# Sums of squares of ten chunks by products of the channels with themselves, instead of Square and add

## The chip, the cores and the metric

The kernel runs on one core of one Trainium2 chip. The metric is the device time of one execution in microseconds. The time before is the median of three runs. One execution was recorded by the hardware profiler, and all rows of the trace below come from that one. A core has TensorE (PE in the rows; PEld is its weight load), VectorE (DVE), ScalarE (ACT), GpSimd (POOL) and SyncE, whose queue (SPq) issues most of the transfers. Each works through its own list of instructions in order, and they wait for one another by semaphores.

## The reference, cut to what matters

```python
B, N, C = 4, 5056, 256
qn = q / (np.linalg.norm(q, axis=1, keepdims=True) + 1e-06)
kn = k / (np.linalg.norm(k, axis=1, keepdims=True) + 1e-06)
s = kn.transpose(0, 2, 1) @ qn / tau
a = softmax of s over its last axis
out = v @ a                        # [B, N, C], then as [B * N, C] into:
logits = x @ w_gate                # one of E = 8 experts for each token
h = np.maximum(xe @ w1[e], 0.0)    # F = 1024
out[mask] = gate_w[mask, None] * (h @ w2[e])
```

For each batch the kernel needs the 256 x 256 product of the channels of k with those of q over all 5056 tokens, and, for the norms, the sum of squares over the tokens of each of the 512 channels of q and k.

## The kernel before

**Attention.** A batch's q and k come in 20 chunks (`nch`) of 256 padded tokens: one chunk is a tile `raw` of 128 partitions x 2 tokens x 512 channels in fp32, 256 of q and 256 of k (L190, L191). For each chunk the two accumulators `sp[0]` and `sp[1]` get the product of k and q (L204 to L216), in one of two ways. A chunk that is not split goes to TensorE as fp32: four matmuls of 128 x 256, each with its own weights (L209). A chunk that is split is first cast by ScalarE to a rounded half (L173), VectorE subtracts that from the chunk for the second half (L174), and eight matmuls of the halves follow (L213, L214). Beside that, ScalarE squares the chunk into `sq` (L202), and VectorE adds `sq` to the running sum `ssq` (L203); of chunk 0 the square goes to `ssq` itself (L200). After the last chunk four small matmuls with a column of ones sum `ssq` over the partitions into `ntp` (L223), VectorE clips it into `ss` (L229), and from it come the norms, the softmax and the 256 x 256 matrix of the batch, with the gate's weights behind it.

Then come ten groups (`G`) of 512 tokens. The values of a group are loaded (`vraw`, L308), eight fp32 matmuls into four tiles `px` give its rows and logits (L322 in the first batch), ScalarE copies each `px` into `xg` and squares it for a scale (L327, L329), ScalarE and VectorE write the rows as two halves (L343, L344), a short chain on VectorE picks the expert (`r_m` to `r_ex`, L352 to L373), TensorE counts places (`rtp`, L380 and L383), and four indirect transfers on POOL's queue scatter the rows to their expert (L402).

**Weights.** `weights()` loads the 16 matrices of the experts (L117, L122; the last into `wraw`), forms the diagonal of a product of each with itself on TensorE for its scale (`gram`, 16 matmuls of 128 x 128 in bf16, L137, and L140 to L144), and splits each in two halves with one large operation on ScalarE (L105) and one on VectorE (L106).

**Blocks.** When the first six groups (`CUT`) of batch 0 are scattered, `table(0)` counts the rows of each expert (`ctp`, L462, and some 25 small operations on VectorE to `c_tb`), and blocks of 256 rows of one expert start. The block's address is read from `c_tb` on SyncE's queue, the rows come by a transposing transfer (`xT`, L543) and their factors by a small one (`mt`, L545, used by VectorE at L586 for `b_fac`); then come 48 matmuls `hp` (L571) and 48 `y` (L594). The rest of the kernel is a row of such blocks, with the attention of the later batches dealt out between them.

**Order of the work.** At L658 to L662 one loop deals out the opening: batch 0 (`first`), the weights, and from step 23 on one chunk of batch 1 (`second`) in every step, ten chunks in all; chunks 10 to 19 of batch 1 run between blocks. Of batch 1, chunk 0 and chunks 14 to 19 are split, 1 to 13 are not. The framework then orders each engine's instructions by its own planning, so that the order on an engine is not that of the code; it is fixed when the program is built.

**Buffers.** Chunks and values of these stages share the three buffers of the tag `raw`; `px` and `gram` share three PSUM buffers (`hp`); `hl`, `sq`, `soft` and `wraw` share two buffers (tag `hl`); `ps_y` holds the two PSUM buffers `y0` and `y1` of a block's result, which batch 0 used for its `sp` before.

Of the kernel before, what the change touches and what calls it, by code (L numbers as in the profile page):

```python
# [10 lines left out]
F32 = mybir.dt.float32  # L11
F32R = mybir.dt.float32r
F16 = mybir.dt.float16
# [3 lines left out]
ALU = mybir.AluOpType  # L17
# [3 lines left out]
P = 128  # L21
# [9 lines left out]
CUT = 6  # L31
# [30 lines left out]
def attention_then_experts(ctx, tc, q, k, vT, tau, w_gate, w1, w2, kc, out):  # L62
    nc = tc.nc
    sync, act, vec, pool, pe = nc.sync, nc.scalar, nc.vector, nc.gpsimd, nc.tensor

    one = ctx.enter_context(tc.tile_pool(name="one", bufs=1))
    work = ctx.enter_context(tc.tile_pool(name="work", bufs=2))
    tiny = ctx.enter_context(tc.tile_pool(name="tiny", bufs=2))
# [3 lines left out]
    ps_y = ctx.enter_context(tc.tile_pool(name="ps_y", bufs=1, space=bass.MemoryType.PSUM))  # L72
# [91 lines left out]
    NATIVE = 14  # L164
# [9 lines left out]
        vec.tensor_tensor(out=hl[:, 1], in0=raw, in1=hl[:, 0], op=ALU.subtract)  # L174
        return hl

    def attention(b, s_split, x_split, acc):

# [1 line left out]
        sp = [pool_.tile([P, 2, C], F32, tag=tag, name=f"sp{c}") for c, (pool_, tag) in enumerate(acc)]  # L182
        ssq = one.tile([P, 2, 512], F32, tag="a_l", name="ssq")
        nch = len(s_split)
        for ch in range(nch):

            tag, bufs = (("raw", RAW), ("rows", 3), ("xg", 2), ("raw", RAW), ("rows", 3))[ch % 5 if b == 0 else 0]
            raw = work.tile([P, 2, 512], F32, tag=tag, name="raw", bufs=bufs)
            sl = slice(2 * ch, 2 * ch + 2)
            sync.dma_start(out=raw[:, :, 0:C], in_=qv[b][:, sl, :])  # L190
            load = sync.dma_start(out=raw[:, :, C:512], in_=kv[b][:, sl, :])  # L191
            if b == 0:
                last_load[0] = load.ins
            if s_split[ch]:
                hl = split(raw)
                sq = raw
            else:
                sq = work.tile([P, 2, 512], F32, tag="hl", name="sq", bufs=2)
            if ch == 0:
                act.activation(ssq, raw, AF.Square)  # L200
            else:
                act.activation(sq, raw, AF.Square)  # L202
                vec.tensor_tensor(out=ssq, in0=ssq, in1=sq, op=ALU.add)  # L203
            for j in range(2):  # L204
                first, last = ch == 0 and j == 0, ch == nch - 1 and j == 1
                for c in range(2):
                    kc0 = C + c * P
                    if not s_split[ch]:
                        pe.matmul(  # L209
                            sp[c][:, 0, :], raw[:, j, kc0 : kc0 + P], raw[:, j, 0:C], start=first, stop=last  # L210
                        )
                        continue
                    pe.matmul(sp[c], hl[:, 0, j, kc0 : kc0 + P], hl[:, :, j, 0:C], start=first, stop=False)  # L213
                    pe.matmul(  # L214
                        sp[c][:, 1, :], hl[:, 1, j, kc0 : kc0 + P], hl[:, 0, j, 0:C], start=False, stop=last
                    )  # L216
            yield 2 * 640

# [2 lines left out]
        tp = ps_t.tile([P, 512], F32, tag="tp", name="ntp")  # L221
# [3 lines left out]
        def four(name):  # L225
            return tiny.tile([P, 4], F32, name=name)

        ss, y, h = four("n_ss"), four("n_y"), four("n_h")
        vec.tensor_scalar(out=ss, in0=tp[:, 0:4], scalar1=1e-30, scalar2=None, op0=ALU.max)  # L229

        vec.tensor_scalar(
            out=y.bitcast(I32), in0=ss.bitcast(I32), scalar1=-0.5, scalar2=float(0x5F3759DF), op0=ALU.mult, op1=ALU.add
# [34 lines left out]
        for c in range(2):  # L267
            vec.scalar_tensor_tensor(
                out=s2[:, c, :], in0=sums[c], scalar=rn[:, 2 + c : 3 + c], in1=rq, op0=ALU.mult, op1=ALU.mult
# [8 lines left out]
        for c in range(2):  # L278
            vec.tensor_scalar(
                out=a_x[:, c, 0:C], in0=s2[:, c, :], scalar1=z[:, c : c + 1], scalar2=None, op0=ALU.mult  # L280
            )

        tp = ps_t.tile([P, 512], F32, tag="tp", name="atp")
# [7 lines left out]
        tp = ps_t.tile([P, 512], F32, tag="tp", name="gtp")  # L291
        for c1 in range(2):
            for c2 in range(2):
                pe.matmul(
                    tp[:, c1 * E : (c1 + 1) * E], aT[:, c2, c1 * P : (c1 + 1) * P], wg[:, c2, :],
                    start=(c2 == 0), stop=(c2 == 1),
# [9 lines left out]
        for g in range(G):  # L306
            raw = work.tile([P, 2, 512], F32, tag="raw", name="vraw", bufs=RAW)
# [4 lines left out]
            ss = tiny.tile([P, T], F32, name="x_ss")  # L312
            for t in range(T):
# [22 lines left out]
                out=sc.bitcast(I32), in0=ss.bitcast(I32), scalar1=-0.5, scalar2=float(0x5F3759DF) + 4.92 * TWO23,  # L336
                op0=ALU.mult, op1=ALU.add,
# [26 lines left out]
            last = g == G - 1  # L364
# [248 lines left out]
    def run(gen):  # L613
        for _ in gen:
            pass
# [8 lines left out]
    normal = [(ps_a, "acc")] * 2  # L624
    wts = weights()
    first = attention(0, [False] * nch, False, [(ps_y, "y0"), (ps_y, "y1")])
    second = attention(1, [i == 0 or i >= NATIVE for i in range(nch)], True, normal)
    take(first, 2)


# [58 lines left out]
    look(0)  # L689
    look(1)  # L690
    run(first)
    for n, (s, i) in enumerate(stages):
        while s not in tables:
            next(side)
        look(n)
        look(n + 1)
        for k, _ in enumerate(block(s, tables[s], i, *ahead.pop(n))):
            if k == 0:
                look(n + 2)
            want = np.interp(n + (k + 1) / 8, marks, amounts)  # L700
            while side is not None and s_at < want:
                ns = next(side, None)
                if ns is None:
                    side = None
                else:
                    s_at += ns
# [41 lines left out]
```

## Time and profile before

| | |
|---|---|
| time, median of 3 runs | 1219.38 us (1216.57 to 1224.59) |
| the profiled execution's own time | 1222.09 us, of it 1220.2 us from the first to the last instruction |
| PE busy | 1161.4 us (95%) |
| PE's weight loads | 1025.4 us (84%) |
| DVE busy | 904.7 us (74%) |
| ACT busy | 645.3 us (53%) |
| POOL busy | 383.5 us (31%) |
| PE's mean granted clock | 0.988 of full speed |

Busy shares are means over the whole span, and the stages differ: the opening, up to about 160 us, holds batch 0's attention, the split of the weights and ten chunks of batch 1, and after it come the blocks. Times in rows of the timeline are counted from the span's start. The matmuls' ends are modelled in the trace, so the spacing of their starts says more than their length does. One fp32 matmul stands in the trace as two records.

### The profile page before, as it was taken

How to read it: one execution, taken by the hardware profiler on the slowest of the kernel's cores; microseconds unless marked ns; L12 is line 12 of the kernel's file. 1: busy time of each engine (PE TensorE's matmuls, PEld its weight loads, DVE VectorE, ACT ScalarE, POOL GpSimd, SP SyncE). 2: the span in 40 equal slices, each digit the busy share in tenths (PEclk: the TensorE clock that was granted, in tenths of full speed). 3: DMA queues.
4: the chain of work that ended last, by engine and by line, in shares of the span. 5: the costliest groups of instructions: out<-in, count | busy, mean ns of one | idle time of the engine just before them, and what ended most of it. 6: DMA issues, size and time to landing. Idle time of an engine off the chain costs nothing. (4 is left out here: it accounts for less than half of the span.)

```text
span 1220.2 us, 28272 instructions
## 1 busy us (share of the span) xinstructions
PE 1161.4 (95%) x10212; PEld 1025.4 (84%) x10212; DVE 904.7 (74%) x2384; ACT 645.3 (53%) x1362; POOL 383.5 (31%) x366
## 2 busy tenths in 40 slices
PE   8888789988899999999999999999999999999998
PEld 7767578877788889888888888889888888888897
DVE  5689789677787777777788777777676656656886
ACT  5388864776655545666655545666523332332322
POOL 0027651444521122444441112444431111111111
PEclk9889999999999999999999999999999999999999
DMA  9989685444355433444354534433241222221221
GB/s 302 351 278 316 156 206 136 117 122 131 103 137 127 136 84 96 119 121 109 94 152 114 138 87 96 114 114 79 62 114 48 53 53 53 49 45 42 43 50 33
DMA packets 196830, 145.91 MB, mean 120 GB/s; under 512 B 117580, under 2 KB 176337, under 8 KB 196688
## 3 DMA queue, kind: packets, MB, share of 16 engines
q1 hardware_dynamic: 181296, 102.48, 34.2%
q0 software_dynamic: 15392, 41.60, 9.5%
q8 instruction: 81, 1.33, 0.5%
q14 instruction: 61, 0.50, 0.1%
HBM read 80.03 MB, written 43.29 MB: 101 GB/s over the span
## 5 line engine op out<-in xcount | busy, mean ns | idle before, releaser
L571 PE MATMUL hp<-xT,wp 128*128 128x256 f16 (+1 forms) x4320 | 452.1, 263 | 5.1 <-issue 1.4
L594 PE MATMUL y<-wp,ht 128*128 128x256 f16 x3888 | 450.3, 273 | 6.4 <-DVE ht L579 2.7
L594 PEld LDWEIGHTS <-ht 128*128 128x128 f16 x3888 | 372.4, 98 | 68.1 <-issue 10.4
L571 PEld LDWEIGHTS <-wp 128*128 128x128 f16 x4320 | 383.8, 98 | 52.1 <-issue 6.1
L605 POOL DMA_INDIRECT out<-o,mt x162 | 184.3, 1138 | 649.6 <-ACT o L603 612.4
L559 DVE COPY wp<-W 128x1024 f16 x720 | 297.6, 428 | 111.9 <-PE y L594 64.4
L578 ACT ACTIVATE ht<-hp 128x512 f16<-128x512 f32 x324 | 191.2, 595 | 201.3 <-PE hp L571 162.8
L579 DVE SCALAR_TENSOR_TENSOR ht<-hp,ht 128x512 f16<-128x512 f32 x324 | 220.4, 685 | 36.8 <-ACT ht L578 31.5
L402 POOL DMA_INDIRECT xs<-rows,r_si x160 | 182.3, 1139 | 145.8 <-ACT xjunk L329 50.1
L603 ACT ACTIVATE o<-y,b_fac 128x256 f32<-128x256 f32 x162 | 68.8, 469 | 175.5 <-PE y L594 161.3
L325 PE MATMUL px<-a_h,hl 128*128 128x264 f32 x480 | 99.1, 296 | 1.3 <-ACT xg L327 0.8
L343 ACT ACTIVATE rows<-xg,x_sc 128x256 f16<-128x256 f32 x160 | 69.2, 498 | 35.7 <-issue 16.3
L325 PEld LDWEIGHTS px<-a_h,hl 128*128 128x128 f32 x480 | 79.1, 188 | 4.1 <-issue 1.8
L174 DVE TENSOR_TENSOR hl<-raw,hl 128x1024 fp32r<-128x1024 f32 x47 | 57.4, 1221 | 30.7 <-ACT hl L173 30.7
L213 PE MATMUL sp<-hl 128*128 128x512 f32 x188 | 72.4, 418 | 1.0 <-DVE hl L174 1.0
L173 ACT CAST hl<-raw 128x1024 fp32r<-128x1024 f32 x47 | 49.1, 1044 | 45.0 <-PE sp L214 40.0
L209 PE MATMUL sp<-raw 128*128 128x256 f32 x264 | 64.0, 394 | 9.0 <-DMA raw<-in_k 9.0
L202 ACT ACTIVATE raw<-raw 128x1024 f32<-128x1024 f32 x44 | 46.6, 1058 | 44.6 <-DVE hl L174 42.5
L344 DVE SCALAR_TENSOR_TENSOR rows<-xg,x_sc,rows 128x256 f16<-128x256 f32 x160 | 69.1, 478 | 0.6 <-issue 0.2
L325 PE MATMUL px<-a_l,hl 128*128 128x264 f32 x240 | 68.6, 286 | 0.0
L329 ACT ACTIVATE xjunk<-xg 128x256 bf16<-128x256 f32 x160 | 66.7, 417 | 3.1
L327 ACT COPY xg<-px 128x264 f32<-128x264 f32 x160 | 57.8, 367 | 14.2 <-PE px L325 6.9
(140 smaller groups left out, 925.6 us busy)
## 6 DMA issues: line engine op xcount, KB each, us to landing
raw<-in_q SPq DMA_DIRECT2D x80, 256.0 KB
raw<-in_k SPq DMA_DIRECT2D x80, 256.0 KB
vraw<-in_vT SPq DMA_DIRECT2D x40, 512.0 KB
W<-in_w SPq DMA_DIRECT2D x30, 512.0 KB
out<-o,mt POOLq DMA_INDIRECT x162
xs<-rows,r_si POOLq DMA_INDIRECT x160
xT<-xs SPq DMA_TRANSPOSE x90
xs<-pad SPq DMA_DIRECT2D x9, 129.0 KB
```

Source lines behind the costliest of these rows:

```text
L213: pe.matmul(sp[c], hl[:, 0, j, kc0 : kc0 + P], hl[:, :, j, 0:C], start=first, stop=False)
L325: pe.matmul(px, hl[:, vh, c, ts], ah[:, c, :], start=(n == 0), stop=(n == 5))
L343: act.activation(r16[:, t, 0:C], x, AF.Copy, scale=sc[:, t : t + 1])
L344: vec.scalar_tensor_tensor(out=r16[:, t, C : 2 * C], in0=x, scalar=sc[:, t : t + 1], in1=r16[:, t, 0:C], op0=ALU.mult, op1=ALU.subtract,)
L402: ins = pool.indirect_dma_start(out=xs[:, :], out_offset=bass.IndirectOffsetOnAxis(ap=si[:n, t : t + 1], axis=0), in_=rows[:n, t, :], in_o ...
L559: vec.tensor_copy(out=t, in_=Wf[:, ds(e * 8192 + n * 1024, 1024)])
L571: pe.matmul(hp[:, f % nf, :], wp[:, dc, wh, (f % 2) * P : (f % 2 + 1) * P], xT[:, 2 * xh + dc, :], start=(n == 0), stop=(n == 5),)
L578: act.activation(ht[:, 0], hp, AF.Relu)
L579: vec.scalar_tensor_tensor(out=ht[:, 1], in0=hp, scalar=0.0, in1=ht[:, 0], op0=ALU.max, op1=ALU.subtract)
L594: pe.matmul(ys[j], hts[f // nf][:, hh, f % nf, j * P : (j + 1) * P], wp[:, f % 2, wh, :], start=(f == 0 and n == 0), stop=(f == 7 and n == 2),
L603: act.activation(o, ys[j], AF.Copy, scale=fac[:, j : j + 1])
L605: pool.indirect_dma_start(out=out[:, :], out_offset=bass.IndirectOffsetOnAxis(ap=mt.bitcast(I32)[:, j, 1:2], axis=0), in_=o, in_offset=Non ...
```

## The change

Batch 1 gets `by_pe` = 2 * CUT - 2 = 10. Of its chunks 0 to 9, ScalarE and VectorE square and add nothing any more. TensorE forms, for each of the two tokens of a chunk's tile and each 128 of the 512 channels, the fp32 product of these channels with themselves into a PSUM tile `own` (buffer `y0`): eight matmuls of 128 x 128 to a chunk, each with its own weights. Chunk 0 is no longer split. Since it now fills only a part of each `sp`, three matmuls with a tile of zeros (`none`) start `own` and both `sp`. Chunk 10 is the first that is squared, into `ssq` itself. After batch 0's groups, `own_sums()` takes the diagonals of `own` with four operations on VectorE, and the sum `gsum` is added where `ss` is formed. 

```diff
--- before.py
+++ after.py
@@ -174,7 +174,20 @@
         vec.tensor_tensor(out=hl[:, 1], in0=raw, in1=hl[:, 0], op=ALU.subtract)
         return hl
 
-    def attention(b, s_split, x_split, acc):
+    gsum = tiny.tile([P, 4], F32, name="n_gs", bufs=1)
+    own = []
+
+    def own_sums():
+
+        for i in range(4):
+            diag = work.tile([P, P], F32, tag="o", name="n_diag", bufs=2)
+            vec.scalar_tensor_tensor(
+                out=diag, in0=own[0][:, i * P : (i + 1) * P], scalar=1.0, in1=ident, op0=ALU.mult, op1=ALU.mult,
+                accum_out=gsum[:, i : i + 1],
+            )
+
+    def attention(b, s_split, x_split, acc, by_pe=0):
+
 
 
 
@@ -194,15 +207,21 @@
             if s_split[ch]:
                 hl = split(raw)
                 sq = raw
-            else:
+            elif ch >= by_pe:
                 sq = work.tile([P, 2, 512], F32, tag="hl", name="sq", bufs=2)
-            if ch == 0:
+            if ch == 0 and by_pe:
+                own.append(ps_y.tile([P, 512], F32, tag="y0", name="own"))
+                none = work.tile([P, 512], F16, tag="o", name="none", bufs=2)
+                vec.memset(none, 0.0)
+                for acc_ in own + [s_.rearrange("p s c -> p (s c)") for s_ in sp]:
+                    pe.matmul(acc_, none[:, 0:P], none, start=True, stop=False)
+            if ch == by_pe:
                 act.activation(ssq, raw, AF.Square)
-            else:
+            elif ch > by_pe:
                 act.activation(sq, raw, AF.Square)
                 vec.tensor_tensor(out=ssq, in0=ssq, in1=sq, op=ALU.add)
             for j in range(2):
-                first, last = ch == 0 and j == 0, ch == nch - 1 and j == 1
+                first, last = ch == 0 and j == 0 and not by_pe, ch == nch - 1 and j == 1
                 for c in range(2):
                     kc0 = C + c * P
                     if not s_split[ch]:
@@ -214,6 +233,12 @@
                     pe.matmul(
                         sp[c][:, 1, :], hl[:, 1, j, kc0 : kc0 + P], hl[:, 0, j, 0:C], start=False, stop=last
                     )
+                for i in range(4 if ch < by_pe else 0):
+                    ch_i = raw[:, j, i * P : (i + 1) * P]
+                    pe.matmul(
+                        own[0][:, i * P : (i + 1) * P], ch_i, ch_i, start=False,
+                        stop=ch == by_pe - 1 and j == 1 and i == 3,
+                    )
             yield 2 * 640
 
 
@@ -226,7 +251,12 @@
             return tiny.tile([P, 4], F32, name=name)
 
         ss, y, h = four("n_ss"), four("n_y"), four("n_h")
-        vec.tensor_scalar(out=ss, in0=tp[:, 0:4], scalar1=1e-30, scalar2=None, op0=ALU.max)
+        if by_pe:
+            vec.scalar_tensor_tensor(
+                out=ss, in0=tp[:, 0:4], scalar=1e-30, in1=gsum, op0=ALU.max, op1=ALU.add
+            )
+        else:
+            vec.tensor_scalar(out=ss, in0=tp[:, 0:4], scalar1=1e-30, scalar2=None, op0=ALU.max)
 
         vec.tensor_scalar(
             out=y.bitcast(I32), in0=ss.bitcast(I32), scalar1=-0.5, scalar2=float(0x5F3759DF), op0=ALU.mult, op1=ALU.add
@@ -624,7 +654,7 @@
     normal = [(ps_a, "acc")] * 2
     wts = weights()
     first = attention(0, [False] * nch, False, [(ps_y, "y0"), (ps_y, "y1")])
-    second = attention(1, [i == 0 or i >= NATIVE for i in range(nch)], True, normal)
+    second = attention(1, [i >= NATIVE for i in range(nch)], True, normal, 2 * CUT - 2)
     take(first, 2)
 
 
@@ -689,6 +719,7 @@
     look(0)
     look(1)
     run(first)
+    own_sums()
     for n, (s, i) in enumerate(stages):
         while s not in tables:
             next(side)
```

The planner gives each engine another order around these. On PE, a chunk that is not split, before (chunk 2; `sp_681` and `sp_682` are the two accumulators, and `gram` is the next matrix's scale):

```order
L209 MATMUL sp_681<-raw 128x256
L209 MATMUL sp_682<-raw 128x256
L209 MATMUL sp_681<-raw 128x256
L209 MATMUL sp_682<-raw 128x256
L137 LDWEIGHTS W
L137 MATMUL gram<-W 128x128
```

The same chunk on PE now (`sp_682` and `sp_683` are the accumulators; x4 counts a row's instructions):

```order
L228 MATMUL sp_682<-raw 128x256
L228 MATMUL sp_683<-raw 128x256
L238 MATMUL own<-raw 128x128 x4
L228 MATMUL sp_682<-raw 128x256
L228 MATMUL sp_683<-raw 128x256
L238 MATMUL own<-raw 128x128 x4
```

Eight products stand in the chunk that were not there, and whatever comes next on PE stands behind them.

On DVE, the first block's `b_fac`, before:

```order
L396 TENSOR_TENSOR r_sl<-rtp,r_ex 128x32
L390 RECIPROCAL rows<-r_z 128x4
L352 TENSOR_REDUCE r_m<-xg 128x4
L399 TENSOR_REDUCE r_si<-r_sl 128x4
L586 ISA
L586 TENSOR_SCALAR b_fac<-mt,fe 128x2
L335 TENSOR_SCALAR x_sc<-x_ss 128x4
L354 TENSOR_TENSOR r_d<-xg,r_m 128x32
```

The same place on DVE now:

```order
L429 TENSOR_REDUCE r_si<-r_sl 128x4
L616 ISA
L616 TENSOR_SCALAR b_fac<-mt,fe 128x2
L387 SCALAR_TENSOR_TENSOR r_eq<-r_d,kt 128x32
L365 TENSOR_SCALAR x_sc<-x_ss 128x4
L389 TENSOR_REDUCE r_r<-r_eq 128x4
L418 TENSOR_REDUCE r_z<-r_d 128x4
L374 SCALAR_TENSOR_TENSOR rows<-xg,x_sc,rows 128x256 x3
L393 TENSOR_TENSOR r_ex<-kt,r_r 128x32
```

Before, the group whose `r_ex` followed the two `b_fac` was group 8, and all 32 `px` matmuls of groups 6 to 9 stood on PE ahead of the `rtp` that needs it. Now the `r_ex` of group 7 follows the first `b_fac` and that of group 8 the second; on PE the `rtp` of group 7 stands behind 24 of the 32 `px` matmuls, five of them follow it, then the `rtp` of group 8, then the last three, then the first half of chunk 10, and then the first block's `hp`.

On the queue of SyncE, the loads ahead of the first block, before:

```order
L308 DMA vraw<-in_vT 128x2x512 x4
L190 DMA raw<-in_q 128x2x256
L191 DMA raw<-in_k 128x2x256
L538 TENSOR_LOAD c_tb
L543 ISA
L543 DMA_TRANSPOSE xT<-xs 128x4x256
```

The same place of that queue now:

```order
L338 DMA vraw<-in_vT 128x2x512 x4
L568 TENSOR_LOAD c_tb
L573 ISA
L573 DMA_TRANSPOSE xT<-xs 128x4x256
L575 ISA
L575 DMA mt<-xs 128x2x2
```

The load of chunk 10 has moved from ahead of the first block's rows to behind the rows and factors of three blocks, where the load of chunk 11 stood before. From the norms of batch 1 on, the orders of PE, DVE and ACT are the same before and now.

## Rows read from the trace of the kernel before

**Rows 1.** Part 1 of the page: busy time, share of the span, instructions
```profile
PE 1161.4 (95%) x10212; PEld 1025.4 (84%) x10212; DVE 904.7 (74%) x2384; ACT 645.3 (53%) x1362; POOL 383.5 (31%) x366
```

**Rows 2.** Busy time by stretch: length, busy per engine (count), granted clock, DMA share, GB/s
```profile
core 0: us, PE busy (x) PEld busy (x) DVE busy (x) ACT busy (x) POOL busy (x), PEclk, DMA share, GB/s
78.20:124.30 46.10, 40.57 (x296) 34.27 (x295) 43.11 (x112) 43.01 (x83) 31.12 (x21) 1.00 0.91 297
124.30:160.20 35.90, 26.72 (x137) 20.09 (x136) 26.85 (x113) 28.41 (x88) 23.74 (x23) 0.90 0.76 192
...
160.20:1220.20 1060.00, 1030.05 (x9428) 916.01 (x9426) 784.40 (x2069) 531.61 (x1137) 327.75 (x318) 1.00 0.37 95
```

**Rows 3.** Timeline of PE, chunks 0 to 9: start, length, what [idle before <-releaser]
```profile
80.31 0.50 PE L213 MATMUL sp<-hl 128*128 128x512 f32 x1 [0.99 <-DVE hl L174]
...
93.80 1.56 PE L209 MATMUL sp<-raw 128*128 128x256 f32 x6 [1.37 <-DMA raw<-in_k]
...
100.86 1.97 PE L209 MATMUL sp<-raw 128*128 128x256 f32 x8 [0.16 <-DMA raw<-in_k]
...
105.91 1.53 PE L209 MATMUL sp<-raw 128*128 128x256 f32 x6 [2.16 <-DMA raw<-in_k]
...
122.88 0.67 PE L209 MATMUL sp<-raw 128*128 128x256 f32 x2 [0.86 <-DMA raw<-in_k]
```

**Rows 4.** Timeline of PE: pairs of starts that give the price of a matmul
```profile
160.19 1.89 PE L209 MATMUL sp<-raw 128*128 128x256 f32 x8
161.92 1.47 PE L571 MATMUL hp<-xT,wp 128*128 128x256 f16 x12
...
199.22 0.95 PE L223 MATMUL ntp<-ones,ssq 128*128 128x1 f32 x8
200.03 2.78 PE L594 MATMUL y<-wp,ht 128*128 128x256 f16 x24
...
204.36 0.71 PE L248 MATMUL ntp<-soft,ones 128*128 128x128 f32 x4 [0.67 <-DVE soft L247]
204.91 4.53 PE L571 MATMUL hp<-xT,wp 128*128 128x256 f16 x40
...
224.88 0.28 PE L325 MATMUL px<-a_l,hl 128*128 128x264 f32 x1
...
225.73 0.40 PE L325 MATMUL px<-a_h,hl 128*128 128x264 f32 x2
```

**Rows 5.** What leaves DVE and ACT: windows of L203 and of L202, timeline
```profile
78.20:160.20 82.00, 12.11 (x10) 0.96 0.85 251
...
78.20:160.20 82.00, 10.53 (x10) 0.96 0.85 251
...
79.03 1.23 DVE L174 TENSOR_TENSOR hl<-raw,hl 128x1024 fp32r<-128x1024 f32 x1
...
77.83 1.05 ACT L173 CAST hl<-raw 128x1024 fp32r<-128x1024 f32 x1
```

**Rows 6.** Timeline of PE from group 5's end to the blocks
```profile
124.28 1.46 PE L209 MATMUL sp<-raw 128*128 128x256 f32 x6
...
133.06 0.18 PE L380 MATMUL rtp<-r_ex,tri 128*128 128x32 f16 x1
...
149.99 1.48 PE L571 MATMUL hp<-xT,wp 128*128 128x256 f16 x12 [0.97 <-DMA xT<-xs]
...
155.77 0.19 PE L380 MATMUL rtp<-r_ex,tri 128*128 128x32 f16 x1 [3.86 <-DVE r_ex L363]
```

**Rows 7.** Timeline of SyncE's queue: start and length of an issue
```profile
118.10 0.47 SPq L191 DMA_DIRECT2D raw<-in_k  x1
...
144.95 2.65 SPq L543 DMA_TRANSPOSE xT<-xs  x1
...
153.95 0.51 SPq L191 DMA_DIRECT2D raw<-in_k  x1
```

**Rows 8.** Timeline of DVE: the first two blocks' factors
```profile
151.04 0.23 DVE L586 TENSOR_SCALAR b_fac<-mt,fe 128x2 f32<-128x2 f32 x1 [3.67 <-DMA mt<-xs]
...
155.39 0.23 DVE L586 TENSOR_SCALAR b_fac<-mt,fe 128x2 f32<-128x2 f32 x1 [1.55 <-DMA mt<-xs]
```

## The prediction

> **What bounds the kernel now.** I read part 1 of the page first, then busy times by stretch, then the timeline of each engine in the stretch that the change touches. Part 1 says that PE is busy for 1161.4 us, 95% of the span [rows 1]. That is a mean over stages, so I cut the span where the work changes: at 78.2 us, just ahead of chunk 0 of batch 1; at 124.3 us, where group 5's `px` matmuls have ended; and at 160.2 us, from where PE has the blocks and nothing more to wait for. Behind 160.2 us PE is busy 1030 of 1060 us [rows 2]: there PE's own list is the time, and the orders there barely differ. So what the change does is decided ahead of 160.2 us, and a delay at that point is carried to the end one for one.
>
> Between 78.2 and 124.3 us three engines are nearly full at once: DVE 43.1, ACT 43.0 and PE 40.6 of 46.1 us [rows 2]. PE's idle time there is five waits, 0.99 + 1.37 + 0.16 + 2.16 + 0.86 = 5.5 us [rows 3], and 46.1 less 5.5 is the 40.6 that the windows show, so it has no other. Four of the five end with a chunk's load. From 124.3 to 160.2 us no engine is full: the chain of group 5's rows, their scatter, `table(0)` and the first block's loads sets the pace, and PE fills it with groups 6 to 9. The waits there that matter are those of PE for `xT` (0.97) and for an `r_ex` that stands behind the two `b_fac` on DVE (3.86) [rows 6, 8].
>
> **What leaves DVE and ACT.** Ten additions, 12.1 us of DVE, and chunk 0's subtraction, 1.2 us; ten squares of about 10.5 us of ACT and chunk 0's cast, 1.05 us [rows 5]. That is 13.3 us and 11.6 us off the two fullest engines of the stretch. It is worth time only if they, and not PE, set the pace afterwards.
>
> **What PE gets.** 10 chunks x 8 = 80 fp32 products of 128 x 128. No such stream is in the trace, so I bound one product. Below: a chunk's four 128 x 256 matmuls take 1.73 us from start to start, 161.92 - 160.19, or 0.433 each [rows 4], and half the columns would be 0.216, if the weights' load stays hidden. Nearest in form: the 128 x 264 matmuls of split values have a weight load of the same shape for each 264 columns streamed at a single rate; seven follow one another in 225.73 - 224.88 = 0.85 us, 0.121 each [rows 4], and an fp32 product of 128 columns stands as two such records: 0.24 us. Two real 128 x 128 fp32 products take 204.91 - 204.36 = 0.55 us, 0.275 each, but with a pipeline to fill [rows 4]. The upper end: products with one column are almost weight load alone, (200.03 - 199.22) / 4 = 0.20 us [rows 4], and 0.20 + 0.216 = 0.42 if load and stream did not overlap. I take 0.24, the row nearest in its alternation of load and stream: 80 x 0.24 = 19.2 us. The ends are 17 and 34 us. The three starting matmuls of 512 columns are 3 x 0.216 = 0.65 us by the same rate. Chunk 0 in fp32 instead of halves I take at nothing, since both forms stream within a few tenths of a microsecond of each other.
>
> What could hide the products is PE's idle time. It was 5.5 us in the first stretch, and DVE's and ACT's relief cannot give more than that. PE becomes the bound there.
>
> The Trainium skill, TensorE: Matmul & The Clock Gate, section Back-to-back issue gap, speaks against this change: in a stream of load and matmul pairs, 128 columns are paid at about 81 ns where streaming alone would be 56. By that ratio a product would be 0.216 x 81 / 56 = 0.31 us, an estimate from the page, and the 80 of them 25 us. The seven matmuls at 0.121 us do not show such a loss; no row here shows the exact shape.
>
> **The sum, up to group 5.** PE's work from 78.2 to 124.3 us was 40.6 us. By the new order chunk 8 and the first quarter of chunk 9 (2.2 us at the rate above) follow group 5 instead of preceding it; 64 products (15.4) and the start (0.65) come in. If the old waits all vanish, group 5 ends at 78.2 + 40.6 - 2.2 + 15.4 + 0.65 = 132.7 us, 8.4 later.
>
> **From group 5 to the blocks.** Behind it PE has chunk 8 (3.65) and a part of chunk 9 (1.6), so `rtp` of group 5 runs at 137.9. From there to the first block's rows being asked for it was 144.95 - 133.06 = 11.9 us, through the scatters [rows 6, 7]: now 149.8. The first `b_fac` came 6.1 us behind that, the second 10.4 us [rows 7, 8]: now 155.9 and 160.2. Here the new order costs something. Group 7's `r_ex` is queued on DVE behind the first `b_fac`, five small operations at about 0.2 us (155.39 to 155.77 held two [rows 6, 8]) and three quarter-size ones at about 0.3 (a quarter of the 1.23 of [rows 5]): 157.9. PE gets to that `rtp` at 132.7 + 7.3 + 24 x 0.446 = 150.7 and stands until 157.9 with eight `px` matmuls, chunk 10 and the blocks behind it. Then five `px`: 160.1; the next `r_ex`, seven operations behind the second `b_fac`: 161.6; three `px`: 162.9. Chunk 10's load has moved behind three blocks' loads on SyncE's queue, to where chunk 11's stood, whose issue ended 9.5 us after the first `xT` was asked for [rows 7]; a load took 4.3 us from the end of its issue to PE's use, 122.88 - 118.57 [rows 3, 7]: 149.8 + 9.5 + 4.3 = 163.6. Then chunk 10 (1.7) and 36 `hp` (4.1 at 4.53 / 40 [rows 4]): 169.4 us, where the trace before has the same work done at 160.2. That is 9.2 us later. The small matmuls of `rtp` are left out. I add a little under 1 us for `px` matmuls that wait for ACT's copies, since eight now stand together on three buffers: 10 us.
>
> `own_sums` adds four operations of 128 x 128 on DVE, under 2 us by the sizes in [rows 5]; `table(0)` is interleaved with them and the scatters end later anyway, so they cost nothing. The first block needs `y0` some 20 us after that.
>
> Against the profiled execution's 1222.09 us this is 1232; that execution lies 2.7 us above the median of its three runs, so I forecast 1219.4 + 10 = 1229.5 us. About 1% (12 us) is what a measurement of this kernel can tell from no change, so this is "within 1%", on the slow side.
>
> **The rivals.**
>
> *Packed.* The wait behind `b_fac` does not come to more than now, because ACT and DVE, relieved, finish group 5's rows and the table sooner. The floor is PE's work: 40.57 + 26.72 [rows 2] + 19.2 + 0.65 = 87.1 us in place of 82.0, +5.1; at full clock in the second stretch (0.90 there now) some 2.7 less, +2.4. So 1222 to 1225 us. For it: the chain was run with ACT and DVE congested. Against: scatter and transfers make up most of those 11.9 us, and the new order puts PE behind them.
>
> *Load not hidden: slower by more than 1%.* If a product's weight load is not covered by the one before, it costs up to 0.42 us. From about 0.28 us each the delay passes 12 us; at 0.35 us group 5 ends 7 us later still and the sum is +17, 1236 us; at 0.42, +21. This is also what the page's ratio would do, at 0.31 us: some +14. Against it stand the seven matmuls at 0.121 us; for it, the 0.275 of the two real products.
>
> *DVE sets the pace: faster.* If PE's rows overstate its work and DVE alone bounds the first stretch, eight chunks at 1.2 us and the subtraction leave it: 46.1 gets 11 us shorter, 1208 us. Against: the waits and busy time of PE add up to the stretch, so PE has no room for 15 us more. It would need products that cost next to nothing.
>
> **How the numbers follow.** Forecast 0.52 (1225 to 1232), packed 0.22, load not hidden 0.20, DVE sets the pace 0.06. The range 1219 to 1239 leaves out the last and the upper part of the third, about 0.14 in all. Slower by over 1%: the third and the top of the first, 0.30; faster by over 1%: 0.06; within 1%: 0.64.
>
> **What would show it.** In the profile after: `own` matmuls of two records, spaced 0.12 us a record; PE's waits for chunk loads gone between 78 and 125 us and DVE and ACT no longer full; group 5's last `px` near 133 us; PE idle for about 7 us on an `rtp` that waits for an `r_ex` behind `mt`; chunk 10's load landing after the first block's rows; the blocks in full flow some 10 us later, and the same length behind that. The prediction is wrong if the stretch behind the blocks' start changes length, if the products are spaced otherwise, or if `px` waits for ACT cost several microseconds.

## The result and the profile after

The changed kernel takes 1233.74 us, the median of four runs (1231.28 to 1235.91), against 1219.22 us for four runs of the kernel before (1216.57 to 1224.59): a ratio of 1.0113, with a 95% interval of 1.0074 to 1.0152. The forecast was 1229.5 us, in a range of 1219 to 1239. The forecast also called the change "within 1%"; here it is 1.13%, and the interval holds 1%.

The profiled execution of after took 1231.28 us, the fastest of its four; that of before took 1222.09 us. So the two traces can explain 9.2 us, which is less than the medians' 14.5 us. Two further comparisons, on other chips, gave 12.5 and 10.7 us (experiments, below): about 1%.

The first view is part 1 of the page after, for [rows 1]:

```profile
PE 1178.2 (96%) x10375; PEld 1044.8 (85%) x10375; DVE 895.9 (73%) x2382; ACT 636.8 (52%) x1351; POOL 375.5 (31%) x366
```

PE has 16.8 us more than before, DVE and ACT about 9 us less each. The busy times by stretch after, cut at the same work as [rows 2]: the end of group 5's `px`, and the point where chunk 10 and 36 `hp` are done. The first row is the stretch of before with its old bounds:

```profile
core 0: us, PE busy (x) PEld busy (x) DVE busy (x) ACT busy (x) POOL busy (x), PEclk, DMA share, GB/s
78.20:124.30 46.10, 44.38 (x355) 39.97 (x353) 32.84 (x90) 32.37 (x66) 29.85 (x20) 1.00 0.87 274
...
78.20:132.70 54.50, 52.33 (x413) 47.05 (x411) 37.92 (x106) 36.97 (x73) 33.93 (x24) 1.00 0.81 255
132.70:170.00 37.30, 30.97 (x185) 25.55 (x185) 23.59 (x123) 26.10 (x87) 18.07 (x21) 0.95 0.72 201
170.00:1229.40 1059.40, 1031.04 (x9424) 917.03 (x9421) 783.88 (x2061) 531.30 (x1137) 322.53 (x316) 1.00 0.36 95
```

In the same 46.1 us DVE fell from 43.1 to 32.8 and ACT from 43.0 to 32.4; only PE is still nearly full. The stretch behind the blocks' start is 1059.4 us, where it was 1060.0 in [rows 2]. All of the delay arises ahead of it.

The timeline of PE after, at the places that the prediction names (start, length, what [idle before <-releaser]):

```profile
81.02 1.03 PE L228 MATMUL sp<-raw 128*128 128x256 f32 x4
81.88 1.05 PE L238 MATMUL own<-raw 128*128 128x128 f32 x8
82.77 1.03 PE L228 MATMUL sp<-raw 128*128 128x256 f32 x4
...
133.19 1.03 PE L228 MATMUL sp<-raw 128*128 128x256 f32 x4
138.75 0.19 PE L410 MATMUL rtp<-r_ex,tri 128*128 128x32 f16 x1 [0.35 <-DVE r_ex L393]
...
155.33 0.19 PE L410 MATMUL rtp<-r_ex,tri 128*128 128x32 f16 x1 [2.22 <-DVE r_ex L393]
...
165.45 0.19 PE L410 MATMUL rtp<-r_ex,tri 128*128 128x32 f16 x1 [1.24 <-PE sp L228]
...
167.99 0.17 PE L492 MATMUL ctp<-r_ex,ones 128*128 128x8 f16 x1 [1.80 <-issue]
...
170.19 1.89 PE L228 MATMUL sp<-raw 128*128 128x256 f32 x8
```

Four products are eight records: 82.77 - 81.88 = 0.89 us, 0.111 a record and **0.2225 us a product**, 17.8 us for the 80. The row at 133.19 starts where group 5's `px` have ended. The row at 170.19 answers to that at 160.19 in [rows 4]: the same work is done 10.0 us later, but for group 9's `rtp` and a `ctp`, which now come ahead of it and before came behind it, about 0.1 us of work.

The waits of PE from 78 to 180 us after (engine, line, waited for: us, times, longest):

```profile
PE rtp L410 <- DVE r_ex L393: 3.8, 4, 2.2
PE ctp L492 <- issue: 1.8, 1, 1.8
PE rtp L410 <- PE sp L228: 1.2, 1, 1.2
PE px L352 <- ACT xg L357: 0.7, 1, 0.7
PE gram L137 <- DVE w_diag L140: 0.7, 1, 0.7
```

A sixth wait, 0.2 us at a `gram`, is left out. No chunk load is among them any more. Before, in [rows 3], four of the first stretch's five waits ended with one.

### The profile page after: what moved, and what is told of

It is laid out like the page before. It is cut to its first block, busy times and chain, and to the rows that moved or that the text cites. A ratio compares the mean times of both kernels' runs of the same rounds, so it can differ in the third digit from the quotient of the medians.

```text
span 1229.4 us, 28567 instructions
## 1 busy us (share of the span) xinstructions
PE 1178.2 (96%) x10375; PEld 1044.8 (85%) x10375; DVE 895.9 (73%) x2382; ACT 636.8 (52%) x1351; POOL 375.5 (31%) x366
## 4 chain that ended last, share of the span: by engine, by line
PE 52%; issue 25%; DVE 7%; POOL 5%; DMA 5%; ACT 3%; SPq 3%; another core or an unknown queue 0%; POOLq 0%; DVEq 0%; ACTq 0%
PE hp L601 20%; PE y L624 17%; PE px L355 7%; POOL out L635 4%; PE sp L232 3%; PE sp L233 2%; DMA xs<-rows,r_si 2%; DVE rows L374 2%; DMA raw<-in_k 1%; POOL xs L432 1%; DVE ht L609 1%; SPq L122 1%; DMA raw<-in_q 1%; SPq L117 1%; DVE wp L589 1%
## 5 line engine op out<-in xcount | busy, mean ns | idle before, releaser
L432 POOL DMA_INDIRECT xs<-rows,r_si x160 | 177.2, 1108 | 151.1 <-issue 47.1
L373 ACT ACTIVATE rows<-xg,x_sc 128x256 f16<-128x256 f32 x160 | 69.1, 497 | 35.7 <-issue 14.5
L173 ACT CAST hl<-raw 128x1024 fp32r<-128x1024 f32 x46 | 48.0, 1043 | 40.1 <-PE sp L233 36.7
```

The costliest lines, as they stand in the source:

```text
L373: act.activation(r16[:, t, 0:C], x, AF.Copy, scale=sc[:, t : t + 1])
L432: ins = pool.indirect_dma_start(out=xs[:, :], out_offset=bass.IndirectOffsetOnAxis(ap=si[:n, t : t + 1], axis=0), in_=rows[:n, t, :], in_o ...
```

## The experiments

**Theory.** PE was close to being the bound of the opening. The products lengthen its list, the little idle time that it had takes up a part of them, and the rest is carried to the end. What DVE and ACT lose is worth nothing. **Rivals.** The products cost little, and the new order around `b_fac` and `rtp` costs the time; or the relief of DVE and ACT gives some of it back.

To compare openings I use one landmark that has the same work ahead of it in these kernels: the start of chunk 14's first product (the first `sp<-hl` of 512 columns behind the blocks' start). Idle is the length less PE's busy time, from 78.2 us to the landmark of one profiled execution each. Ratios are to the kernel before on the same chip; of the rows behind after, the first four, the next four and the last three were each measured on one chip. The ratios compare all runs and are not quotients of the medians beside them. A landmark is missing where the work ahead of it differs; in the others PE's `hp`, `y`, `rtp` and `ctp` up to it are equal in number, and up to 16 of 136 `gram` matmuls, under 1 us, already lie ahead of 78.2 us in some.

| kernel | median us | ratio [95% interval] | landmark us | PE busy us | PE idle us |
|---|---|---|---|---|---|
| before | | | 173.31 | 80.39 | 14.7 |
| after | 1233.74 | 1.0113 [1.0074, 1.0152] | 183.16 | 96.46 | 8.5 |
| after, again | 1243.73 | 1.0092 [1.0063, 1.0121] | 183.88 | 96.30 | 9.4 |
| cheap products | 1230.24 | 0.9992 [0.9975, 1.0009] | 171.16 | 83.99 | 9.0 |
| no products | 1248.49 | 1.0141 [1.0108, 1.0174] | | | |
| both sums | 1242.68 | 1.0100 [1.0070, 1.0130] | 186.82 | 97.05 | 11.6 |
| after, `b_fac` late | 1234.17 | 1.0075 [1.0051, 1.0100] | 189.59 | 98.43 | 13.0 |
| before, `b_fac` late | 1222.68 | 0.9981 [0.9964, 0.9999] | 173.47 | 79.73 | 15.5 |
| cheap products, `b_fac` late | 1224.21 | 0.9982 [0.9959, 1.0006] | 173.50 | 85.41 | 9.9 |
| no products, sum doubled | 1225.15 | 1.0003 [0.9985, 1.0021] | 173.86 | 81.59 | 14.1 |
| after, third chip | 1243.79 | 1.0087 [1.0056, 1.0118] | 186.19 | 96.86 | 11.1 |
| twice the products | 1255.80 | 1.0189 [1.0158, 1.0220] | 198.66 | 114.31 | 6.2 |
| five chunks | 1239.31 | 1.0064 [1.0038, 1.0090] | 182.15 | 91.45 | 12.5 |

The landmarks come from the windows of each trace. Two of them, of before and then of after:

```profile
78.20:173.31 95.11, 80.39 (x533) 65.79 (x531) 80.92 (x258) 78.11 (x178) 63.51 (x48) 0.96 0.85 243
```

```profile
78.20:183.16 104.96, 96.46 (x694) 84.08 (x692) 74.59 (x273) 69.61 (x166) 58.84 (x49) 0.98 0.75 224
```

PE's busy time grew by 16.1 us, its idle time fell by 6.2 us, and the landmark moved by the difference, 9.9 us.

### After, on a second and a third chip

The changed kernel, unchanged.

> The changed kernel, once more, in five rounds. The profiled pair differs by 9.2 us (1231.28 against 1222.09), the medians by 14.5. If the change is worth what the stretch before the blocks shows (blocks in full flow at 170.2 instead of 160.2 us), the rounds give a ratio of 1.007 to 1.010; if something beyond that stretch varies from execution to execution, 1.011 to 1.015, and the second profile shows where.

> The changed kernel on the chip of the next two, as the point between them: ratio 1.008 to 1.012. Theory (PE's work in the opening, less what its waits there take up) and rival (a fixed price of the new order) expect the same here.

Measured: 1.0092 and 1.0087, both inside the first interval. The loss is 12.5 and 10.7 us on these chips; with the first comparison's 14.5 the change costs 0.9 to 1.1%. The landmark differs between executions of this one kernel: 183.2, 183.9 and 186.2 us. A landmark of a single execution is therefore good to 2 or 3 us, and so are differences of PE's idle time between single executions.

### Cheap products

The products are formed from the upper halves of the fp32 numbers, read as bf16, and the diagonals are multiplied by 1.0054 for the bits left out. The code puts them in the same places, but the planner makes another order of it.

```diff
                     ch_i = raw[:, j, i * P : (i + 1) * P]
+                    top = raw.bitcast(BF16)[:, j, 1::2][:, i * P : (i + 1) * P]
...
-                        own[0][:, i * P : (i + 1) * P], ch_i, ch_i, start=False,
+                        own[0][:, i * P : (i + 1) * P], top, top, start=False,
```

> Products from the upper halves of the fp32 values, read as bf16, times a constant for what the cut takes; everything else as in the changed kernel, and the order on PE nearly the same. One product should cost 0.06 us instead of 0.22, 80 of them 4.6 instead of 17.8. Theory (PE's work is the price): group 5 ends about 10 us earlier than in the changed kernel, and the time falls back to 1215 to 1223, at or below before. Rival (the new order at the first block, with chunk 10's load and an r_ex behind other waits, is the price): the time stays within 4 us of the changed kernel, at 1229 or more.

Measured: 0.9992 [0.9975, 1.0009]; the loss is gone. The timeline of PE in this kernel:

```profile
124.37 0.39 PE L239 MATMUL own<-raw 128*128 128x128 bf16 x4
124.60 1.08 PE L228 MATMUL sp<-raw 128*128 128x256 f32 x4
...
150.29 0.19 PE L411 MATMUL rtp<-r_ex,tri 128*128 128x32 f16 x1 [4.21 <-DVE r_r L390]
```

Four products take 124.60 - 124.37 = 0.23 us, 0.057 each, so 80 of them 4.6 us in place of 17.8. PE still stands 4.2 us at an `rtp` at 150 us. Against "after, again" on the same chip the products are 13.2 us cheaper, the median is 13.5 us lower and the landmark 12.7 us earlier, with PE's idle time nearly equal (9.0 and 9.4 us).

This run alone doesn't tell the products' time from the order around them, since the order changed too. On SyncE's queue the load of chunk 10 stands ahead of the first block's rows again, as it did before, and not behind them as in after:

```profile
136.93 0.46 SPq L204 DMA_DIRECT2D raw<-in_k  x1
143.21 1.36 SPq L574 DMA_TRANSPOSE xT<-xs  x1
```

The kernel with twice the products, below, keeps after's order.

### No products, two attempts

The products, `own_sums` and the addition of `gsum` are taken out, the rest of the change stays: no squares and additions for ten chunks, chunk 0 unsplit.

```diff
                 for i in range(4 if ch < by_pe else 0):
                     ch_i = raw[:, j, i * P : (i + 1) * P]
-                    pe.matmul(
-                        own[0][:, i * P : (i + 1) * P], ch_i, ch_i, start=False,
-                        stop=ch == by_pe - 1 and j == 1 and i == 3,
-                    )
+                    pass
...
     run(first)
-    own_sums()
```

> No products at all: the sums of squares of chunks 0 to 9 are left out, on PE as on ACT and DVE (the norms of batch 1 then cover ten chunks only). This is what the relief of ACT and DVE alone is worth. Theory: PE had 5.5 us of waits in that stretch and some 9 behind it, so 3 to 8 us, 1211 to 1216. Rival (DVE and ACT set the pace, so that their 13 us come off): 1206 to 1208.

Measured: 1.0141, slower than after. This answers nothing about the opening: with norms from a part of the chunks the rows of batch 1 fall to blocks in another way, and there are three more blocks (93 `b_fac` in the trace, 90 before). Part 1 of its page, beside 10212 instructions on PE before:

```profile
PE 1183.5 (95%) x10430; PEld 1043.4 (84%) x10430; DVE 909.8 (73%) x2407; ACT 641.9 (52%) x1360; POOL 376.1 (30%) x369
```

A kernel whose work depends on its data can't have a sum left out like that. The second attempt doubles the sum of the chunks that are left, which brings the number of blocks back (10214 instructions on PE):

```diff
-            vec.tensor_scalar(out=ss, in0=tp[:, 0:4], scalar1=1e-30, scalar2=None, op0=ALU.max)
+            vec.tensor_scalar(out=ss, in0=tp[:, 0:4], scalar1=1e-30, scalar2=2.0 if by_pe else 1.0, op0=ALU.max, op1=ALU.mult)
```

> No products and no squares of chunks 0 to 9, as before, but the sum over the other ten chunks is doubled, so that the norms of batch 1 are nearly right and the tokens go to the experts in nearly the numbers of the reference. The run without that had three blocks of the rest more than the others (10430 matmuls on PE where 10215 were due), so its 17 us were not the opening's. In its trace the blocks were in full flow at 160.4 us. Theory: what DVE and ACT give up alone is worth nothing to little at the first block, ratio 0.997 to 1.001. Rival (their 13 us come off): 0.989 to 0.993.

Measured: 1.0003 [0.9985, 1.0021]. To the landmark its DVE is busy 73.3 us where before shows 80.9, and its ACT 70.8 where before shows 78.1, and nothing comes of it. The timeline of its PE shows where the gain was lost:

```profile
145.59 1.94 PE L344 MATMUL px<-a_x,vraw 128*128 128x264 f32 x8
153.05 0.21 PE L402 MATMUL rtp<-r_ex,tri 128*128 128x32 f16 x1 [5.52 <-issue]
...
155.10 2.21 PE L593 MATMUL hp<-xT,wp 128*128 128x256 f16 x12
```

Group 5's `rtp` runs at 130.71 us in place of 133.06 [rows 6], and PE reaches those of the later groups sooner too, but stands 5.5 us at group 8's, ahead of the first `hp` at 155.10; before, the first `hp` ran at 149.99 [rows 6]. What an earlier group 5 won was given back at a later wait. This kernel too has an order of its own, so it shows that the relief gained nothing here, and not that it could gain nothing in any order.

### Both sums

The products are added and the squares and additions are kept as well; `gsum` is formed and not used.

```diff
-            elif ch >= by_pe:
+            else:
                 sq = work.tile([P, 2, 512], F32, tag="hl", name="sq", bufs=2)
...
-            if ch == by_pe:
+            if ch == 0:
                 act.activation(ssq, raw, AF.Square)
-            elif ch > by_pe:
+            else:
                 act.activation(sq, raw, AF.Square)
```

> The products are added, and the squares and additions of chunks 0 to 9 are kept (chunk 0 unsplit as in the changed kernel). Theory: PE is the bound with the products in it, so the squares beside them cost little: within 4 us of the changed kernel, 1229 to 1238. Rival (what ACT and DVE give up is what keeps the change from costing the products' whole 18 us): 1238 to 1246.

Measured: 1.0100 [1.0070, 1.0130] beside 1.0092 for after on the same chip, with a median 1 us lower (1242.68 against 1243.73): not resolved. With the products on PE no difference was measured between DVE and ACT doing their old work and leaving it.

### Twice the products, and half of them

Each product is formed twice, and the diagonal is halved:

```diff
+                    for rep in range(2):
+                        pe.matmul(
+                            own[0][:, i * P : (i + 1) * P], ch_i, ch_i, start=False,
+                            stop=ch == by_pe - 1 and j == 1 and i == 3 and rep == 1,
+                        )
```

> Each product is formed twice, and the diagonals are halved: 80 more products of 0.22 us, 17.8 us of PE, with nothing else changed. Theory (PE is the bound in the opening once the first ten chunks' products are in it, so that each further one is paid in full): 15 to 19 us above the changed kernel, ratio to before 1.021 to 1.026. Rival (a fixed price of the new order, products mostly hidden): less than 9 us above it, 1.010 to 1.017.

In the other, five chunks in place of ten:

```diff
-    second = attention(1, [i >= NATIVE for i in range(nch)], True, normal, 2 * CUT - 2)
+    second = attention(1, [i >= NATIVE for i in range(nch)], True, normal, 5)
```

> Only chunks 0 to 4 have their sums from PE: 40 products, 8.9 us, and 0.65 for the start. Theory: PE's 5.5 us of waits in that stretch and a little behind it take up most, 1 to 4 us above before, ratio 1.001 to 1.004. Rival (a fixed price of the new order): as the changed kernel, 1.008 or more.

Measured: twice 1.0189, 12.0 us over after on the same chip; five 1.0064, 4.5 us under it. The landmarks say the same, 12.5 us later and 4.0 us earlier than after's 186.2. Both times fell outside what the theory expected, and outside what the rival expected too, between the two; the intervals reach into the ranges of both. The direction held; the rule "idle time fills first, and the rest is carried" did not hold as a sum over the whole opening. The windows to the landmark, of twice and of five:

```profile
78.20:198.66 120.46, 114.31 (x844) 100.82 (x841) 75.07 (x268) 67.72 (x164) 56.99 (x49) 0.99 0.68 195
```

```profile
78.20:182.15 103.95, 91.45 (x599) 77.12 (x598) 78.02 (x266) 73.51 (x169) 60.66 (x48) 0.93 0.73 223
```

Twice adds 80 x 0.2225 = 17.8 us of products. PE is busy 17.45 us longer than in after on the same chip and idle 4.9 us less (11.1 to 6.2), which gives the 12.5.

Twice is also the run that holds the order fixed where the rival sees the price: from the first `ctp`, behind the last product, to the landmark PE's instructions are the same in the same order as in after. The windows ahead of that `ctp` and behind it, of "after, third chip" and then of twice:

```profile
78.20:141.25 63.05, 60.53 (x471) 54.41 (x470) 43.95 (x124) 42.07 (x88) 35.24 (x25) 1.00 0.77 243
141.25:186.19 44.94, 36.33 (x228) 29.48 (x226) 32.31 (x151) 28.80 (x81) 24.88 (x25) 0.96 0.67 182
```

```profile
78.20:156.98 78.78, 77.82 (x617) 71.41 (x615) 44.70 (x118) 40.81 (x85) 35.76 (x28) 1.00 0.63 198
156.98:198.66 41.68, 36.49 (x229) 29.41 (x226) 30.36 (x150) 26.91 (x79) 21.24 (x22) 0.96 0.77 190
```

Ahead of the `ctp` the second 80 products cost 15.7 of their 17.8 us, with PE's idle time down from 2.5 to 1.0 us: there PE is the bound and pays nearly in full. Behind it 3.3 us come back, with the same work and the same order. That stretch took 42.2 us in the first execution of after and 44.9 in this one, so a single pair doesn't show whether the 3.3 us are due to the products, and the medians, 12.0 us apart with intervals of about 4 us to either side, don't decide it.

Five adds 8.9 us of products and 0.65 for the start to before's list, yet its idle time is 12.5 us where before had 14.7, and its mean granted clock is 0.93 where before had 0.96. The planner makes another order for each number of chunks, and in this one the waits moved and did not shrink: 3.7 us for `r_ex`, 1.9 each for `vraw` and `xg`, 1.8 for a chunk's load.

### `b_fac` behind the block's last `ht`

In the prediction PE stood behind an `r_ex` that stood on DVE behind the first block's `b_fac`. Here `b_fac` is issued only after the block's last `ht`, in after, in before, and in the kernel with cheap products:

```diff
-                vec.scalar_tensor_tensor(
+                last_ht = vec.scalar_tensor_tensor(
...
-        fac = tiny.tile([P, 2], F32, name="b_fac")[:, 0:nj]
-        vec.tensor_scalar(out=fac, in0=mt[:, :, 0], scalar1=fe[:, ds(e, 1)], scalar2=None, op0=ALU.mult)
...
+        with tc.issue_after(last_ht.ins):
+            vec.tensor_scalar(out=fac, in0=mt[:, :, 0], scalar1=fe[:, ds(e, 1)], scalar2=None, op0=ALU.mult)
```

> The changed kernel with the block's b_fac kept on DVE behind the block's last ht, so that no r_ex stands behind a wait for mt. Theory (the products on PE cost some 9 us up to group 5's end, and the wait behind b_fac costs 2 to 4 more): 2 to 5 us below the changed kernel, ratio to before 1.004 to 1.008. Rival (the wait behind b_fac takes the place of a wait for xT that comes anyway): no difference to the changed kernel, ratio 1.009.

> The kernel before with b_fac kept behind the last ht. PE's wait of 3.86 us for an r_ex behind two b_fac should go. Theory: 2 to 4 us faster than before, ratio 0.997 to 0.998. Rival (the next wait, for xT or for ht, takes its place): 1.000.

> Products of the upper halves in bf16, and b_fac behind the last ht. Top_half alone had the blocks in full flow at 157.0 instead of 160.2 us, with a wait of 4.2 us on PE for an r_ex behind b_fac left. Theory: both add, 3 to 6 us below before, ratio 0.995 to 0.998. Rival (what is won in the opening is given back behind it): 0.999 to 1.000.

Measured: 1.0075, 0.9981 and 0.9982. After's intervals with and without the edit overlap, so a gain of it there is not resolved. Before gains 0.2% [0.0%, 0.4%]; the cheap products' interval reaches past 1. But PE's wait at that `rtp` did not go. In before it was 3.86 us [rows 6] and with the edit it is 5.41 us, since DVE now stands elsewhere ahead of the `r_ex`:

```profile
156.66 0.21 PE L380 MATMUL rtp<-r_ex,tri 128*128 128x32 f16 x1 [5.41 <-DVE r_ex L363]
```

```profile
156.07 0.43 DVE L559 COPY wp<-W 128x1024 f16 x1 [5.49 <-remote]
```

So the edit was worth a few tenths of a per cent at most, and it doesn't price the wait behind `mt`: another wait took its place. Before with this edit is the only kernel here that is faster than before beyond its interval, and barely. The timeline of DVE, ACT and PE in after with `b_fac` late:

```profile
170.50 0.43 DVE L589 COPY wp<-W 128x1024 f16 x1 [7.05 <-remote]
...
170.50 0.60 ACT L608 ACTIVATE ht<-hp 128x512 f16<-128x512 f32 x1 [6.34 <-remote]
...
171.11 0.21 PE L410 MATMUL rtp<-r_ex,tri 128*128 128x32 f16 x1 [6.12 <-DVE r_ex L396]
```

DVE and ACT both stand still until 170.50 us, with a releaser that the trace calls remote, and PE waits 6.1 us behind them. So this execution (one of the slower of that kernel, 1237.13 us of 1230.6 to 1240.4) has the latest landmark but one in the table.

## Why the prediction was right, step by step

**PE becomes the bound of the first stretch: right.** The waits for chunk loads are gone, DVE and ACT are no longer full, and group 5 ends at 133.19 us where 132.7 was forecast. PE still waits 2.2 us in there (54.50 - 52.33), where none was assumed; the 64 products, cheaper than forecast by 64 x 0.0175 = 1.1 us, made up for half of it, and the rest of PE's work was shorter too. That DVE and ACT had nothing to give is borne out by the kernel without products (1.0003) and by that with both sums (1.0100), each in its own order. The rival in which DVE sets the pace falls with them.

**The price of a product: a little too high.** 0.24 us was forecast from matmuls of split values; it is 0.2225, near the lower bound of 0.216 that came from half of a 256-column matmul. So 17.8 us in place of 19.2. The rival in which the weights' load is not hidden falls: it needed 0.28 us or more. Its forecast of some 14 us, met by the first comparison's 14.5, came near by chance. The Trainium skill, TensorE: Matmul & The Clock Gate, section Back-to-back issue gap, by whose ratio a product would have been 0.31 us, is not borne out: the measured 0.111 us a record decides, and the bf16 products of the same shape took 0.057 us where that section has 0.081.

**The start and the blocks: right.** The three starting matmuls took 0.65 us as forecast (80.37 to 81.02 us), and the stretch behind the blocks' start kept its length.

**The wait at group 7's `rtp`: mis-sized.** 7.2 us was forecast and 2.2 us measured. PE came later than 150.7 us: group 5's end (0.5 us), the `rtp` matmuls that were left out, two short waits and `px` matmuls somewhat slower than 0.446 us put it at about 153.1. DVE came sooner than 157.9: the first block's rows were asked for at 148.65 and not 149.8, and its `b_fac` followed 3.8 us behind that and not 6.1; from there to the `r_ex` it took about 0.9 us longer than forecast, of it 0.61 a wait for ACT's `rows`. The timelines of SyncE's queue and of DVE after, for [rows 7, 8]:

```profile
148.65 1.36 SPq L573 DMA_TRANSPOSE xT<-xs  x1
...
155.99 0.47 SPq L204 DMA_DIRECT2D raw<-in_k  x1
```

```profile
152.47 0.23 DVE L616 TENSOR_SCALAR b_fac<-mt,fe 128x2 f32<-128x2 f32 x1 [1.65 <-DMA mt<-xs]
...
156.44 0.23 DVE L616 TENSOR_SCALAR b_fac<-mt,fe 128x2 f32<-128x2 f32 x1 [0.35 <-issue]
```

The other waits in that stretch were 1.8 us at a `ctp`, 1.2 at a later `rtp`, 0.7 for `xg` and 0.35 at group 5's `rtp`. From group 5's end to the 36 `hp` PE was idle 37.30 - 30.97 = 6.3 us.

**PE's work behind group 5: too small, and that is why the sum came out.** From 132.7 to 169.4 us the forecast has 36.7 us, of it 7.2 + 1.5 + 0.7 = 9.4 us of waits (group 7's and group 8's `r_ex`, chunk 10's load) and so 27.3 us of work, with a little under 1 us added for `px`. Measured, from 133.19 to 170.19 us, it is 37.0 us: 0.35 + 0.73 + 2.22 + 1.24 + 1.80 = 6.3 us of waits and 30.7 of work. The work was 3.4 us more than forecast: the small matmuls of `rtp` and `ctp` were left out, and nothing was put in for a lower clock, where the mean granted clock was 0.95; 5% of 37.3 us are 1.9 us, an estimate. The waits were 3 to 4 us less. The two errors cancel. The sum of 10.0 us, forecast and measured, is right by luck in this stretch; the delay up to group 5, 8.4 us forecast and 8.9 measured, rests on the mechanism that was forecast, PE as the bound.

**Packed, the rival nearest to it, falls.** Its 1222 to 1225 us wanted PE's idle time up to the blocks to vanish: 82.0 - 67.3 = 14.7 us before [rows 2]. After, 2.2 and 6.3 us of it are left, 8.5 in all.

**From the trace to the medians.** The sum was made between two executions, and there it comes out within a microsecond. The median of after lies 4 us above the forecast and 2 us above the 1225 to 1232 us that the forecast's own chance covered, and those of the three comparisons 14.5, 12.5 and 10.7 us above before, where 10 was forecast: a ratio of 1.0087 to 1.0113, on either side of the 1% that the forecast named. Executions of one kernel differ by 3 us in the opening alone.

**Open.** The theory that PE's added work is carried to the end, less what idle time it fills, is shown by twice, where the order behind the last product is after's, and agrees in its direction with five and the cheap products, whose orders differ. How much idle time it fills was not predictable: 6 us with ten chunks, 2 with five, 5 more with the products doubled. No experiment here separates the order from the amount of work at five chunks, and none gives the order of after without the products, so a part of its loss may be due to the order.

## What to carry to other kernels

Work moved to the engine that is already 95% busy is paid for in large part, even where the two engines it leaves are as busy in that stretch. Here 10.7 to 14.5 us were lost for 18.45 us of added matmuls, and 12.0 for a further 17.8: six to eight tenths. Read the idle time of the receiving engine in that stretch, and count the rest as loss. Freed time on the engines beside it was worth nothing here while PE's list did not get shorter: the products at a quarter of the price lost nothing, and no products at all gained nothing. Before a run with one part changed is read as that part's price, compare the orders that the planner made. And don't take a sum that came out for proof of its terms: here a wait forecast 5 us too long and work forecast 3.4 us too short hid one another.

## What was not expected of the hardware

**A product of 128 columns, each with a weight load of its own, loses next to nothing to the load**: 0.2225 us in fp32 and 0.057 us in bf16, about a half and an eighth of the 0.433 us of a 256-column fp32 matmul [rows 4].

**A wait of 2.2 us cost as much clock as one of 3.9.** The windows of 2 us around the wait at `rtp`, of before, which had stood for 3.86 us [rows 6], and then of after, which had stood for 2.22:

```profile
156.00:158.00 2.00, 2.00 (x14) 1.44 (x11) 1.51 (x10) 0.92 (x3) 0.55 (x1) 0.50 0.97 315
158.00:160.00 2.00, 2.00 (x14) 1.51 (x13) 1.41 (x3) 1.80 (x6) 1.56 (x2) 0.64 1.09 363
160.00:162.00 2.00, 2.00 (x13) 1.69 (x11) 2.00 (x8) 1.61 (x3) 1.53 (x2) 1.00 0.98 337
```

```profile
156.00:158.00 2.00, 2.00 (x6) 1.49 (x6) 1.06 (x7) 1.42 (x7) 1.16 (x3) 0.50 0.97 241
158.00:160.00 2.00, 2.00 (x12) 1.53 (x11) 0.82 (x8) 2.00 (x8) 1.57 (x2) 0.68 1.03 323
160.00:162.00 2.00, 2.00 (x12) 1.63 (x11) 1.97 (x8) 1.90 (x9) 1.51 (x2) 1.00 0.78 285
```

The granted clock is 0.50 of full speed, 1.2 GHz, behind both, and back at 1.00 by 160 us in both. Not every wait of that length has this behind it: before, PE waited 2.16 us for a chunk's load up to 105.91 us [rows 3], and the clock was 1.00 over that whole stretch [rows 2]. Before had a second place where the clock fell, here in its windows, behind a wait of 2.9 us for `vraw` that ended at 128.6 us:

```profile
128.00:130.00 2.00, 1.38 (x3) 1.09 (x4) 1.86 (x8) 2.00 (x3) 1.39 (x3) 0.68 0.81 171
130.00:132.00 2.00, 2.00 (x6) 1.57 (x5) 2.00 (x2) 2.00 (x5) 2.00 (x1) 0.50 0.66 247
```

After, PE has products to do at that time, the load is in before it asks, and the clock is 1.00 over the first stretch, up to 132.70 us. By the mean clocks, 0.96 of 95.1 us and 0.98 of 105.0, some 1.7 us less were lost to it, an estimate; that goes most of the way from the 18.45 us of added matmuls to the 16.1 by which PE's busy time grew.

**DVE and ACT stop together at a block's start.** The stops that end with "remote", at a block's first `wp` copy and first `ht`, come in several kernels: in before with `b_fac` late both engines stood until 156.07 us, DVE for 5.5 and ACT for 4.8 us. What releases them is not in the trace, and no experiment here was made on it.
